# Products of ones through the first search of a linear-attention and balanced-expert kernel, with an older order of its attention loop

## The chip, the cores and the metric

The kernel runs on one core of a Trainium2 chip, in one launch. The metric is the device time of that launch in microseconds (us), compared by the median of several runs. A profile of one execution stands beside it. Engines are named as in the profile: PE (matrix products), DVE (vector), ACT (scalar), POOL (GpSimd) and SP, whose queue issues most transfers.

## The reference, cut to what matters

```python
# attention: q, k, v are (8, 8, 576, 64)
kv  = np.einsum('bhsd,bhse->bhde', k, v)
out = np.einsum('bhsd,bhde->bhse', q, kv)
rms = np.sqrt(np.mean(out * out, axis=-1, keepdims=True) + 1e-06)
x   = (out / rms * g_norm).transpose(0, 2, 1, 3).reshape(4608, 512)

# experts: w_gate (512, 8), w1 (8, 512, 1024), w2 (8, 1024, 512), cap = 576
logits = x @ w_gate
order = np.argsort(-logits.flatten())
for idx in order:                       # the best pair of token and expert first
    tok, e = idx // 8, idx % 8
    if assigned[tok] >= 0 or counts[e] >= cap: continue
    assigned[tok] = e; counts[e] += 1
for e in range(8):
    out[assigned == e] = np.maximum(x[assigned == e] @ w1[e], 0) @ w2[e]
```

Each expert takes exactly 576 tokens. Which ones is decided greedily over all pairs, so an expert's rows are known only when a threshold on the logits has been found at which it is full.

## The kernel before, in words

**Attention** (`prepare`, `tiles`). There are eight batches. `load` issues k, v and q of a batch in halves (`h`) of 576 KB on SP's queue; `paced` makes each load wait for the third one before it. `prepare(b)` is a generator with four or five parts, which makes what the tiles of batch `b` need: `sum_kv(r)` multiplies k and v of one pair of heads into `kv_ps` (four values of r), ACT and DVE bring the sum to `kv`, POOL copies it to `kvx`, PE turns it round (`t_ps`), ACT copies that to `kvt`, PE multiplies it with the gate (`w_ps`) and DVE copies the result into `kvx`. `turn_q(n)` (n from 0 to 4) transposes q into `qt`, copied from PSUM by DVE for n = 1 and 2 and by ACT otherwise. `again` issues the load for batch b + 2 into the buffers that have come free.

The main loop goes over the batches. A batch has four tiles of 128 tokens, an odd one also the tile that is split between it and the batch before. `one(t)` makes a tile: sixteen records of products into `o_ps` (two buffers), ACT squares it and copies it to `o_sb`, DVE sums the squares. After each tile comes the next part of `prepare(b + 1)`, so PE's order is tile, part, tile, part. `scale` and `logits` then give the norm and the logits of the batch; POOL scales the rows into `xo`, except those of the last batches (`own` false), which ACT scales after the loop (`late`, L529). `writes` holds the transfers of `xo` to `x_dram`. Here they are issued behind batches 4 and 5 and at the end. `chore` does pieces of the search's set-up (`early`) between tiles. In this stretch the orders of PE, DVE, ACT and SP are those of the program.

`ones(n)` gives PE n products of ones, 128x128 by 128x512 in bf16, whose result nobody reads. `warm(n)` is the same in the second pool of PSUM. Before, `ones` stands at the start (18), in batch 0's preparation (2, 6, 5), before `kv_ps` (2) and before some tiles of the first batches; `warm` stands behind the list of the first expert (20) and between its transposes.

**The first search** (`threshold(0)`, `assign_first`, `fetch(0)`). Six steps narrow the threshold. In each, PE counts, in 36 small products (L665), how many tokens are over each of 32 candidates; DVE finds the first full expert's place (L679, L681); PE adds it over the partitions (L686, "the number"); DVE makes from it the next midpoint (L691), for the first steps digits (L316) and comparisons (L322), later candidates (L708) and comparisons (L336), in three thirds, so that PE can begin on the first. `lowest` puts two products more (L630, L633) behind the number in two of the steps. `assign_first` then adds up who is taken (L748, L763), `fetch(0)` makes the list of rows (L931 to L950), POOL gathers them from `x_dram` (L971), PE transposes them (L1063) and the first expert's products begin (L1161).

**The experts.** For each expert the products of both layers, with the next expert's search interleaved in a planned order. The change does not touch this.

Of the kernel before, what the change touches and what calls it, by code (L numbers as in the profile page):

```python
# [26 lines left out]
def kernel(  # L27
# [63 lines left out]
    for b, order in enumerate(("kvqkvq", "kvkvqq")):  # L91
        for n, name in enumerate(order):
            load(name, b, int(name in order[:n]))
# [274 lines left out]
    def prepare(b):  # L368
# [4 lines left out]
        qt = att.tile([P, 2, NT, HP], FT, name="qt", tag="qt", bufs=2)  # L373
# [25 lines left out]
        def again(names, h):  # L399
            if b + 2 < B:  # L400
                for name in names:
                    load(name, b + 2, h)

        turns = [[0], [1], [2], [3], [4]] if b == 0 else [[], [0], [1, 2], [3], [4]]

        def turn_some():
            for n in turns.pop(0):
                turn_q(n)
                if n in (2, 4):
                    again("q", n // 2 - 1)  # L410

        if b > 0:
            ones(2, kv_ps[:, 0, :])
        sum_kv(0)
        sum_kv(1)
        again("kv", 0)
        if b == 0:
            ones(2)
        turn_some()
        yield  # L420
        if b == 0:
            ones(6)
# [10 lines left out]
        kvx = att.tile([P, H, W], FT, name="kvx", tag="kvx", bufs=2)  # L433
        for n in range(2):
            nc.gpsimd.tensor_copy(kvx[n * D:(n + 1) * D, :, 0:D], kv.rearrange("p r l d -> p (r l) d"))
        turn_some()
# [3 lines left out]
        if b + 1 == B:  # L440
            ones(3)
# [5 lines left out]
        turn_some()  # L447
        yield
        turn_some()
# [10 lines left out]
        turn_some()  # L460

    HELD = 6
    writes, late = [], []
    last_own = GC - R

    def tiles(c0, rows):
# [4 lines left out]
        xo = att.tile([P, T, H, D], FT, name="xo", tag="xo", bufs=HELD)  # L471
# [5 lines left out]
        def one(t, copies, fill, wait):  # L477
# [22 lines left out]
            if not wait:  # L500
                while copies:
                    copies.pop(0)()
# [39 lines left out]
    with tc.manual_schedule(engines={PE, DVE, ACTE, SPE}):  # L542
        ones(18)
        for _ in prepare(0):
            pass
        for b in range(B):
            parts = prepare(b + 1) if b + 1 < B else iter(())
            rows = [((b, j), (b, j + 2)) for j in (0, 1, 4, 5)]
            if b % 2:
                rows.append(((b - 1, R - 1), (b, R - 1)))  # L550
            one, scale, logits = tiles(b // 2 * R + b % 2 * (R // 2), rows)
            copies = []
            if b in choose_at:
                early(*choose_at[b])
            order = range(len(rows)) if b % 2 == 0 else [len(rows) - 1] + list(range(len(rows) - 1))
            for n, t in enumerate(order):
                one(t, copies, 1 if b < 3 and n in (0, 3) else 0, b + 1 == B and n == len(rows) - 2)
                next(parts, None)
                if b < 2 or b == 6 or n in (1, 3):
                    chore()  # L560
            for _ in parts:
                pass
            if b + 1 == B:
                while chores:
                    chore()
            scale()
            logits()
            if b < 4:
                chore()

            while b in (B - 4, B - 3) and writes:
                writes.pop(0)()
        early(27, GC)
        while chores:
            chore()
        for do in late:
            do()
        while writes:
            writes.pop(0)()
# [35 lines left out]
    for n, x in enumerate((-0.5, 1.0 / QP, 0.0)):  # L615
        nc.vector.memset(one_more[:, n:n + 1], x)

# [35 lines left out]
    def threshold(t, over, width, inv, mid):  # L653
# [3 lines left out]
        for s in range(NSTEP):  # L657
# [4 lines left out]
            if first:  # L662

                for c in range(GC):
                    nc.tensor.matmul(n_ps[0:QP, :, 0],  # L665
                                     lhsT=over[c // THIRD][:, c % THIRD],
                                     rhs=best[:, :, c], start=(c == 0), stop=(c == GC - 1))
            else:
                for c in range(0, GC, G):
                    nc.tensor.matmul(n_ps, lhsT=over[:, c:c + G].rearrange("p c n -> p (c n)"), rhs=best[:, :, c:c + G],  # L670
                                     start=(c == 0), stop=(c == GC - G))
# [14 lines left out]
            nc.tensor.matmul(kk, lhsT=ones_b, rhs=some, start=True, stop=True)  # L686
            exact = s + 1 >= DIGITS
# [45 lines left out]
    def assign_first(ends):  # L733
# [14 lines left out]
        nc.tensor.matmul(all_ps[:, 0:2].rearrange("p t e -> p (t e)"), lhsT=ones_b, rhs=sums, start=True, stop=True)  # L748
        edge = small("edge", GC)
# [13 lines left out]
        nc.tensor.matmul(all_ps[:, 2, 0:1], lhsT=before, rhs=turn_of[:, GC - 1:GC], start=True, stop=True)  # L763
        nc.vector.tensor_tensor(room, room, all_ps[:, 0], op=AL.subtract)
# [137 lines left out]
    def warm(times):  # L902
        w_ps = psm.tile([P, 512], FT, name="warm_ps", tag="y", bufs=2)
        for _ in range(times):
            nc.tensor.matmul(w_ps, lhsT=ones_b, rhs=wide, start=True, stop=True)

    def fetch(t, which, index, later):
# [25 lines left out]
        nc.tensor.matmul(a_ps[:, GC + 1:GC + 2], lhsT=prior, rhs=along[:, GC - 1:GC], start=True, stop=True)  # L933
        kn = know[:, t % 2]
# [16 lines left out]
        if t == 0:  # L951

            warm(20)
# [391 lines left out]
```

## Time and profile before

| what | us |
|---|---|
| median of 3 runs (650.66 to 658.63) | 651.92 |
| the profiled execution's own time | 650.66 |
| its span in the profile | 648.9 |
| PE busy in the span | 601.2 |
| DVE busy | 380.6 |
| POOL busy | 387.0 |
| ACT busy | 202.3 |
| last attention tile, start of its products | 113.61 |
| first count of the search's last nine columns (L665) | 121.68 |
| numbers (L686) of the six steps | 122.53, 125.37, 128.22, 131.07, 134.66, 138.78 |
| products of the list (L950) | 145.51 |
| first transposes of gathered rows (L1063) | 151.32 |
| first expert product (L1161) | 155.57 |

Times of instructions are counted from the start of the span. A line of the timeline gives the start, the duration, the engine, the line of the kernel, the operation, what it writes and reads, and in brackets how long the engine was idle before it and what ended that. Durations of single products on PE include their drain, so successive ones overlap, and what a product costs PE is the distance to the next one's start.

### The profile page before, as it was taken

Reading aid. Unit: us, or ns where it says so; the run is one execution under the profiler, and the core shown is the slowest. Engines: PE = TensorE matmul, PEld = TensorE weight load, DVE = VectorE, ACT = ScalarE, POOL = GpSimd, SP = SyncE. Lnnn points to the kernel's source line nnn. Section 1 sums busy time; section 2 is a strip of 40 time slices with the busy share of each in tenths; the row PEclk is TensorE's granted clock in tenths of the full one; section 3 lists DMA queues with packets and bytes.
Section 4 is the critical chain, followed back from the end, with each engine's and each line's share of the span. In section 5 each row is a group of like instructions: output and inputs, shape, how many; then the busy total and the mean of one; then the engine's idle time right before and its main releaser. Section 6 shows DMA issues by size and latency. Waiting matters only on the chain.

```text
span 648.9 us, 12775 instructions
## 1 busy us (share of the span) xinstructions
PE 601.2 (93%) x4918; PEld 464.2 (72%) x4932; DVE 380.6 (59%) x1242; ACT 202.3 (31%) x429; POOL 387.0 (60%) x403
## 2 busy tenths in 40 slices
PE   7889899438999999999999999999999999999993
PEld 4677777325787678777867786778678777867873
DVE  4466658767887678479658857966762052132101
ACT  1565656922321232123222312230233123122310
POOL 1136433006775598479738973877498579849822
PEclk9999999559999999999999999999999999999998
DMA  8999997428109105320821091017104420910001
GB/s 272 299 319 307 308 310 294 169 79 261 66 7 325 60 15 202 131 74 2 289 76 42 5 328 41 34 55 277 42 34 156 176 73 1 316 57 34 0 10 65
DMA packets 49884, 91.02 MB, mean 140 GB/s; under 512 B 3744, under 2 KB 20128, under 8 KB 49824
## 3 DMA queue, kind: packets, MB, share of 16 engines
q1 hardware_dynamic: 43200, 71.31, 32.0%
q0 software_dynamic: 5920, 18.88, 8.5%
q8 instruction: 39, 0.64, 0.4%
q14 instruction: 21, 0.17, 0.1%
q10 hardware_dynamic: 704, 0.02, 0.1%
HBM read 71.32 MB, written 18.87 MB: 139 GB/s over the span
## 4 chain that ended last, share of the span: by engine, by line
PE 78%; DVE 8%; issue 5%; DMA 4%; ACT 3%; POOL 2%; POOLq 0%; SPq 0%; DVEq 0%; ACTq 0%
PE x_ps L1161 13%; PE x_ps L1121 12%; PE z_ps L1161 9%; PE y_ps L1161 9%; PE y_ps L1121 8%; PE z_ps L1121 7%; PE o_ps L492 4%; PE y_ps L1223 4%; PE t_ps L1063 3%; DMA v_sb<-in_v_dram 3%; PE kv_ps L396 2%; PE qt_ps L381 2%; PE given_ps L670 1%; PE given_ps L665 1%; ACT sq L498 1%
## 5 line engine op out<-in xcount | busy, mean ns | idle before, releaser
L1166 ACT COPY h<-x_ps 128x288 f32<-128x288 f32 x93 | 37.2, 400 | 165.8 <-PE x_ps L1161 157.8
L1161 PE MATMUL x_ps<-xs,sw 128*128 128x288 f32 x248 | 71.4, 409 | 0.3 <-DVE xs L1076 0.3
L1088 POOL DMA_INDIRECT out_dram<-y_sb,outs x32 | 31.5, 985 | 57.5 <-DVE y_sb L1259 41.7
L1121 PE MATMUL x_ps<-tw,sh 128*128 128x256 f32 x256 | 61.7, 384 | 0.0
L1161 PEld LDWEIGHTS x_ps<-xs,sw 128*128 128x128 f32 x248 | 46.1, 190 | 13.3 <-issue 0.9
L1068 ACT ACTIVATE xt<-t_ps,g_col 128x512 f32<-128x512 f32 (+3 forms) x41 | 25.8, 635 | 91.3 <-PE t_ps L1063 83.6
L524 POOL TENSOR_TENSOR xo<-o_sb,inv 128x512 f32<-128x512 f32 x27 | 28.4, 1081 | 40.3 <-DVE inv L511 40.3
L1113 POOL TENSOR_TENSOR sh<-hid 128x512 f32<-128x512 f32 x32 | 40.7, 1271 | 19.7 <-ACT hid L1136 19.7
L1121 PEld LDWEIGHTS x_ps<-tw,sh 128*128 128x128 f32 x256 | 47.0, 190 | 7.5 <-issue 1.5
L1049 POOL TENSOR_TENSOR sw<-w_sb 128x256 f32<-128x256 f32 x64 | 46.9, 733 | 7.6 <-PE z_ps L1161 7.3
L1136 ACT ACTIVATE hid<-hid 128x576 f32<-128x576 f32 x64 | 43.8, 686 | 22.8 <-DVE hid L1175 12.6
L971 POOL DMA_INDIRECT xg<-x_dram,ids x40 | 38.0, 950 | 15.4 <-issue 9.9
L1199 POOL TENSOR_TENSOR tw<-w_sb 128x512 f32<-128x512 f32 x32 | 40.0, 1273 | 6.9 <-DMA w_sb<-in_moe_w_dram 6.9
L492 PE MATMUL o_ps<-kvx,qt 64*128 64x72 f32 (+1 forms) x640 | 39.2, 271 | 1.0 <-ACT o_sb L499 0.6
L492 PEld LDWEIGHTS o_ps<-kvx,qt 64*128 64x128 f32 (+1 forms) x640 | 34.1, 177 | 6.4 <-issue 4.5
L1161 PE MATMUL z_ps<-xt,sw 128*128 128x288 f32 x128 | 38.0, 414 | 0.0
L1161 PE MATMUL x_ps<-xt,w_sb 128*128 128x288 f32 x124 | 37.3, 415 | 0.6 <-ACT xt L1068 0.6
L503 DVE TENSOR_REDUCE ms<-sq 128x8 f32<-128x512 f32 x36 | 24.4, 683 | 22.3 <-ACT sq L498 22.2
L1161 PE MATMUL y_ps<-xt,w_sb 128*128 128x288 f32 x128 | 36.8, 408 | 0.0
L1161 PE MATMUL z_ps<-xs,sw 128*128 128x288 f32 x128 | 36.8, 409 | 0.0
L1161 PE MATMUL y_ps<-xs,w_sb 128*128 128x288 f32 x128 | 36.5, 407 | 0.0
L1253 ACT COPY u<-x_ps 128x512 f32<-128x512 f32 x24 | 14.0, 584 | 67.3 <-PE x_ps L1121 52.6
(307 smaller groups left out, 1324.5 us busy)
## 6 DMA issues: line engine op xcount, KB each, us to landing
w_sb<-in_moe_w_dram SPq DMA_DIRECT2D x32, 512.0 KB
w_sb<-in_moe_w_dram SPq DMA_DIRECT2D x8, 2048.0 KB
k_sb<-in_k_dram SPq DMA_DIRECT2D x16, 576.0 KB
v_sb<-in_v_dram SPq DMA_DIRECT2D x16, 576.0 KB
q_sb<-in_q_dram SPq DMA_DIRECT2D x16, 576.0 KB
x_dram<-xo SPq DMA_DIRECT2D x16, 512.0 KB
x_dram<-xo SPq DMA_DIRECT2D x4, 256.0 KB
xg<-x_dram,ids POOLq DMA_INDIRECT x40
```

The lines of the kernel that those rows point to most:

```text
L492: nc.tensor.matmul(o_ps[rows_at, rp, (2 * r2 + l) * W:(2 * r2 + l + 1) * W], lhsT=turned_q[bn][ks, l, block // 2:block // 2 + m].rearrange ...
L524: nc.gpsimd.tensor_tensor(xo[:, t], o_sb[:, t, :, 0:D], inv[:, t * H:(t + 1) * H].rearrange("p (h o) -> p h o", o=1).to_broadcast([P, H, D ...
L971: tokens = nc.gpsimd.indirect_dma_start(out=xg[0:nr], out_offset=None, in_=x_dram, in_offset=bass.IndirectOffsetOnAxis(ap=ids[0:nr, n:n + ...
L1049: in_order(nc.gpsimd.tensor_tensor(o, x, y, op=op))
L1088: put = nc.gpsimd.indirect_dma_start(out=out, out_offset=bass.IndirectOffsetOnAxis(ap=ids_of[t][0:nr, n:n + 1], axis=0), in_=y_sb[0:nr, :] ...
L1113: in_order(nc.gpsimd.tensor_tensor(o[:, ms], x[:, ms], y[:, ms], op=op))
L1121: nc.tensor.matmul(p_ps[:, n], lhsT=left[:, f, n * P:(n + 1) * P], rhs=right[:, f], start=first, stop=(f == FH - 1), skip_group_check=True)
L1136: nc.scalar.activation(both, both, ACT.Relu)
L1161: nc.tensor.matmul(p_ps, lhsT=lhs[:, r], rhs=rhs[:, r], start=(m in (1, 2, 4, 5) and r == 0), stop=(r == 1), skip_group_check=(m in (6, 7, ...
L1166: nc.scalar.copy(u, p_ps)
L1199: in_order(nc.gpsimd.tensor_tensor(o, x, y, op=AL.subtract))
L1223: nc.tensor.matmul(y_ps[l * nr:(l + 1) * nr], lhsT=hid[:, l * FH + f, a:a + nr], rhs=w2[:, l * FH + f, :], start=(f == 0), stop=(f == FH - 1))
```

## The change

It does two things. In the first search it puts products of ones wherever PE waits: seven behind the last attention tile, ten between the first 27 counts and the last nine, four behind each number and nine behind the last, three and five within the assignment, two behind the first products of the list and 24 in place of 20 behind the list. And it takes the attention loop in another order: the split tile comes last in its batch and not first; q of a batch is turned one part earlier, with one half of `kv_ps` per part (so `qt` and `kvx` have three buffers); every batch has one product of ones before its first tile and two before its fourth; batch 1 is loaded in the order k, v, q; the writes of x are issued behind each batch as soon as eight are pending; and only the last batch is scaled late by ACT.

```diff
-    for b, order in enumerate(("kvqkvq", "kvkvqq")):
-        for n, name in enumerate(order):
-            load(name, b, int(name in order[:n]))
+    for b in range(2):
+        for h in range(2):
+            for name in "kvq":
+                load(name, b, h)
...
-        turns = [[0], [1], [2], [3], [4]] if b == 0 else [[], [0], [1, 2], [3], [4]]
...
         if b > 0:
             ones(2, kv_ps[:, 0, :])
-        sum_kv(0)
-        sum_kv(1)
-        again("kv", 0)
-        if b == 0:
-            ones(2)
-        turn_some()
-        yield
-        if b == 0:
-            ones(6)
+        for r in range(2):
+            sum_kv(r)
+            if r:
+                again("kv", 0)
+            turn_q(r)
+            yield
         sum_kv(2)
         sum_kv(3)
         again("kv", 1)
...
-        turn_some()
         if b == 0:
             ones(5)
         yield
-        if b + 1 == B:
-            ones(3)
+        turn_q(2)
+        again("q", 0)
         t_ps = psa.tile([P, NP, D], FT, name="t_ps", tag="tr", bufs=2)
...
-        turn_some()
         yield
-        turn_some()
+        turn_q(3)
...
-        turn_some()
-
-    HELD = 6
+        turn_q(4)
+        again("q", 1)
+
+    LAG = 4
     writes, late = [], []
-    last_own = GC - R
+    last_own = GC - (R + 1) // 2
...
-            order = range(len(rows)) if b % 2 == 0 else [len(rows) - 1] + list(range(len(rows) - 1))
-            for n, t in enumerate(order):
-                one(t, copies, 1 if b < 3 and n in (0, 3) else 0, b + 1 == B and n == len(rows) - 2)
+            for t in range(len(rows)):
+                one(t, copies, {0: 1, 3: 2}.get(t, 0))
                 next(parts, None)
-                if b < 2 or b == 6 or n in (1, 3):
+                if b < 2 or t == 3 or b == 6 and t == 2:
                     chore()
             for _ in parts:
                 pass
             if b + 1 == B:
+                ones(7)
                 while chores:
                     chore()
             scale()
             logits()
-            if b < 4:
-                chore()
-
-            while b in (B - 4, B - 3) and writes:
+            if b < B - 1:
+                chore(2 if b == 6 else 1)
+
+            while len(writes) >= 2 * LAG:
                 writes.pop(0)()
...
+    def warm(times):
+        w_ps = psm.tile([P, 512], FT, name="warm_ps", tag="y", bufs=2)
+        for _ in range(times):
+            nc.tensor.matmul(w_ps, lhsT=ones_b, rhs=wide, start=True, stop=True)
...
                 for c in range(GC):
+                    if s == 0 and c == 27:
+                        warm(10)
                     nc.tensor.matmul(n_ps[0:QP, :, 0],
...
             nc.tensor.matmul(kk, lhsT=ones_b, rhs=some, start=True, stop=True)
+            if first:
+                warm(9 if last else 4)
...
         nc.tensor.matmul(all_ps[:, 0:2].rearrange("p t e -> p (t e)"), lhsT=ones_b, rhs=sums, start=True, stop=True)
+        warm(3)
...
         nc.tensor.matmul(all_ps[:, 2, 0:1], lhsT=before, rhs=turn_of[:, GC - 1:GC], start=True, stop=True)
+        warm(5)
...
+        if t == 0:
+            warm(2)
...
         if t == 0:
 
-            warm(20)
+            warm(24)
```

## The prediction

> **What bounds the kernel now.** I read the page's slices first, for the stages and the granted clock.
>
> ```profile
> span 648.9 us, 12775 instructions
> ...
> PE   7889899438999999999999999999999999999993
> ...
> DVE  4466658767887678479658857966762052132101
> ...
> PEclk9999999559999999999999999999999999999998
> ```
>
> A slice is 16.2 us. Slices 1 to 7 are the attention (to about 115 us), the two with clock 5 are the first search, and the rest is the experts' products, which the change leaves alone: everything it can win or lose lies before the first expert product at 155.57. So I take the part before in batches, and then in steps of the search. PE alone in the timeline, over the end of one attention batch:
>
> ```profile
> 65.91 0.66 PE L381 MATMUL qt_ps<-ident,q_sb 128*128 128x128 f32 x4
> 67.19 0.66 PE L381 MATMUL qt_ps<-ident,q_sb 128*128 128x128 f32 x4 [0.62 <-ACT kvt L446]
> 67.77 1.11 PE L492 MATMUL o_ps<-kvx,qt 64*128 64x72 f32 x16
> 68.82 0.66 PE L381 MATMUL qt_ps<-ident,q_sb 128*128 128x128 f32 x4
> 69.41 0.65 PE L456 MATMUL w_ps<-gw,kvt 128*64 128x16 f32 x16
> 70.44 0.44 PE L381 MATMUL qt_ps<-ident,q_sb 128*128 128x128 f32 x2 [0.39 <-DVE kvx L458]
> ```
>
> From start to start a tile costs 1.05 us, four turns of q 0.585, w_ps 0.60, t_ps 0.39, half of kv_ps 0.655 a pair. Apart from two waits (0.62 and 0.39) PE is never idle: a batch of four tiles is 4x1.05 + 2.62 + 2.64 + 0.39 + 0.60 + 0.47 (two products of ones) = 10.9, and with the waits 11.9. The first tiles of batches 4 and 5 stand at 71.85 and 83.77, 11.92 apart. From batch 2 on the attention is bound by PE, and each product put in PE's queue costs its time.
>
> The search is a ring between DVE and PE:
>
> ```profile
> 125.37 0.16 PE L686 MATMUL given_ps<-some,ones_b 128*128 128x3 bf16 x1 [0.43 <-DVE some L681]
> ...
> 125.58 0.28 DVE L691 TENSOR_SCALAR mid<-given_ps,cells,mid 128x1 f32<-128x1 f32 x1 [0.26 <-PE given_ps L686]
> 125.89 0.32 DVE L316 TENSOR_SCALAR digit<-mx,mid,inv 128x72 bf16<-128x72 f32 x1
> 126.24 0.90 DVE L322 TENSOR_TENSOR over_c<-digit,marks 128x384 bf16<-128x384 bf16 x3
> 126.65 1.03 PEld L665 LDWEIGHTS <-over_c 128*32 128x32 bf16 x36 [1.10 <-DVE over_c L322]
> ```
>
> Between the number (L686) and the next counts (L665) PE has 1.28 us free; that is the gap the new products fill. The clock, by the microsecond (columns PE, PEld, DVE, ACT, POOL, granted clock, DMA share, GB/s):
>
> ```profile
> 112.00:113.00 1.00, 1.00 (x20) 0.92 (x18) 0.93 (x2) 0.64 (x3) 0.00 (x0) 1.00 1.01 371
> 113.00:114.00 1.00, 0.62 (x13) 0.48 (x10) 0.69 (x1) 1.00 (x3) 0.00 (x0) 1.00 1.01 371
> 114.00:115.00 1.00, 1.00 (x14) 0.84 (x12) 0.69 (x1) 0.06 (x1) 0.00 (x0) 0.62 1.01 371
> ...
> 148.00:149.00 1.00, 1.00 (x5) 0.40 (x4) 0.87 (x5) 0.00 (x0) 0.85 (x1) 0.81 0.60 193
> ```
>
> It falls at 114.25, while PE is still working, and is back at 148.38, some 2.3 us into the twenty products of ones.
>
> **What the half clock costs now: little.** PE's counts start 27 ns apart in the search and 25 ns apart (L670) at full clock; from the last count to the DVE instruction behind it is 0.21 us in both, and from L686 to L691 0.20 against 0.21 to 0.24. So a full clock saves 36 x 2 ns = 0.07 in each of three steps on digits, nothing in the steps through L336, where DVE's thirds of 0.50 us set the pace, 0.1 at the first count, and 0.4 at the last attention tile (1.44 us at 113.61 against 1.05). That is 0.7 at most. The gathers are not helped: the ones behind the list now end at about the time the first rows land (transposes from 151.3), and 24 x 0.216 = 5.2 us from 145.86 end at 151.1.
>
> **Attention, part by part.** (1) The loop's order. In the changed one tile 0 is followed by half of kv_ps and one turn, tile 1 likewise, tile 2 by kv_ps 1.31, tile 3 by turn 2, t_ps, turn 3, w_ps, turn 4. The last stretch has nothing to lie beside in a batch of four. With tile 3's end as zero: turn 2 to 0.585, t_ps to 0.975; ACT does the square (0.17), the copy (0.66), then kvt (1.19 to 1.56), so turn 3 runs from 1.62 to 2.2, w_ps to 2.8, turn 4 waits for ACT's copy of turn 3 (2.35 to 2.95) and ends at 3.3. In a batch of five the split tile stands behind t_ps: turn 3 from 1.98, w_ps to 3.15, turn 4 behind DVE's kvx (3.43 to 3.64) to 4.0.
> (2) Ones. 0.31 us before tile 0, 0.47 before tile 3, 0.47 before kv_ps, by their rows' starts (46.24 to 46.56; 97.73 to 98.20). Before, only batches 0 to 2 had fills.
> Sums: four tiles 0.31 + 4x1.05 + 0.47 + 4x0.655 + 2x0.585 + 0.47 + 3.3 = 12.54; five 13.24. The old ones, from first tile to first tile, for batches 1 to 6: 13.3, 12.6, 13.0, 11.92, 12.98, 12.05. Differences -0.06, -0.06, +0.24, +0.62, +0.26, +0.49.
> (3) Loads. q is turned one step earlier, and for batch 2 that meets the load: the SP queue issues load n once n-3 has landed, and by that q's first half lands at about 35.9 where the new order wants it at 34.6: +1.3. Later loads are ahead by 2 us or more. In batch 0, with k, v, q in that order and no 2 + 6 ones at its start, the first tile of batch 1 comes 0.85 earlier (v lands at 25.8; kv_ps, ones, tile, 3.3: 32.1 against 32.94).
> (4) Writes. Three x writes of 512 KB go to the SP queue ahead of batch 7's six loads; at 305 GB/s these 1.6 MB move the landing of q's first half from about 94.5 (read off the issue three places behind it) to 99.6, and it is wanted at 100.8. Hidden by 1.2 us; what of that is missing would go on the path.
> (5) Batch 6's scaling moves from ACT (32 x 0.24 = 7.7 us behind 116.86) to POOL (4 x 1.05), idle there. ACT's tail is not on the chain: x lands at 137, the gathers start at 147.88. Nothing.
> (6) Batch 7 is paced by ACT's two passes per tile; its full clock saves 0.2 of the 0.4 above.
> Sum for the attention: -0.85 - 0.06 + 1.3 - 0.06 + 0.24 + 0.62 + 0.26 + 0.49 - 0.2 = +1.7. Bounds: without the load stall and with the loop-end waits (0.85 a batch of four, 0.55 of five) all hidden -3.8; with batch 7 two us late +4.
>
> **The new products in the search.** At full clock one is 0.216 us and all fit: 4 are 0.86 of 1.28, 9 are 1.94 of 2.8 (138.78 to 141.56), 3 are 0.65 of 1.40, 5 are 1.08 of 1.74, 2 are 0.43 of 0.8. Then they cost nothing and save 0.5. At half clock (0.43 each) 4 take 1.72, and the counts start 0.53 late; 9 delay L748 by 1.2, 5 delay L931 by 0.5; the lowest logit's products (L630, L633) then stand on the path, 0.3 each.
>
> Which clock? The window that lost it, from 110.84 to 114.25, held 47 records of o_ps and nothing else. That is 2.9 tiles of 1.05 us on 64 of the array's 128 rows: 0.45 of the array. In the search 0.86 us of full products in a step of 2.85 is 0.30, and between the ten products at the start and the next counts are over 2 us with none. By that row the clock falls again within the first two steps. Once it is at half, 1.72 + of 3.4 us are busy, and it may return: it came back with 0.8, and stayed down with 0.2 (counts alone). I take it to toggle, half of the price: 0.53 x 1.5 + 0.3 + 0.6 + 0.25 - 0.4 = +1.5; bounds -0.5 and +3.8.
>
> The Trainium skill, TensorE: Matmul & The Clock Gate, Part 1, What's actually happening, names an idle window of about 3.4 us as what throttles PE; by it no gap here is long enough, the clock would hold and the sum would be that of the first rival. The fall at 114.25 with PE at work speaks against it as the whole rule.
>
> **Total.** +1.7 + 1.5 = +3.2 on the profiled execution's 650.66, 653.9. That run is the lowest of three; I add the same to their median, 651.92: 655.1, put at 655.0.
>
> **Rivals.**
> The clock holds through the search: +1.7 - 0.5 = +1.2, 653.1. For it: PE is busy in some way in nearly every microsecond of the steps. Against it: the window at 110.84.
> Faster: the waits at the end of each batch disappear, because ACT and DVE reach kvt and qt sooner than I let them. Price 3 x 0.85 + 3 x 0.55 = 4.2, attention -2.5; with the clock held -3.0, 648.9; with it toggling -1.0. It decides from the point where more than 3.2 of the 4.2 is hidden. For it: ACT is busy only 7 of 12 us a batch. Against it: in a batch of four nothing else stands in PE's queue.
> DMA becomes the bound: writes among the loads make batch 7 wait 2 to 3 us, and all else as forecast: 657.5. For it: DMA share 0.92 to 0.96 to 95 us. Against it: the 1.2 us of slack and PE's slower batches.
>
> **How the numbers follow.** Forecast 0.50, clock holds 0.25, faster 0.15, DMA 0.10. The forecast's own range is 652 to 658; to the rivals and the runs' own spread it is 649 to 660. Two per cent, about what this kernel's measurement can tell, is 13 us, and no case reaches it: faster 0.01, within 0.96, slower 0.03.
>
> **What would show it.** First tiles of batches 2, 4, 6 at about 46.65, 72.4, 98.2 (before 46.24, 71.85, 96.75), the last attention product 1.7 later than 115.05, waits of PE for kvt and qt at each batch's end, one wait for q near 35. Granted clock 1.00 past 115 and falling between 121 and 126; PE waiting for nothing between L686 and the counts where it is half. I am wrong if the clock stays 1.00 to the gathers, if the batches are shorter than before, or if anything behind the first expert product moves against its start by over 1 us.

## The result, and the profile after

The changed kernel takes 660.26 us (median of 22 runs, 657.33 to 669.57), the kernel before 651.53 on the same chips: ratio 1.0139, interval 1.0115 to 1.0162, about 9 us. A second set of four runs gave 658.08, ratio 1.0137 (1.0120 to 1.0153). The forecast was +3.2 us, 655.0; the measured median lies just above the upper end of its range, 660.0. Ratios and intervals, here and below, leave out executions that took over 1.5% longer than the fastest of the same kernel; medians and ranges have all. Two executions were profiled: the first took 663.41 us (span 661.5), the second, called `after_again` below, 656.76 (span 654.9). The median lies between them.

The slices of the first profile:

```profile
span 661.5 us, 12874 instructions
...
PE   7989999688999999999999999999999999999994
...
DVE  4456667767688588568757956975782053123201
...
PEclk9979999858999999999999999999999999999998
```

Three things differ in the row of the clock: a 7 in the third slice, inside the attention; an 8, a 5 and an 8 where before had two 5s (the clock comes and goes around the search); and the search lies half a slice later. PE is busy 24 us longer (625.2 against 601.2); its products of ones take 23 us longer (42.7 against 19.7).

Milestones, in us from the start of the span:

| | before | after | after_again |
|---|---|---|---|
| first tile of batch 2 | 46.6 | 49.9 | 46.3 |
| first tile of batch 4 | 71.8 | 75.9 | 72.2 |
| first tile of batch 6 | 96.7 | 101.6 | 98.0 |
| first tile of batch 7 | 108.8 | 114.3 | 110.7 |
| end of the last tile | 115.05 | 123.11 | 120.00 |
| start of the last nine columns of the first count | 121.68 | 130.73 | 127.95 |
| first and last number | 122.53, 138.78 | 131.57, 149.10 | 128.79, 145.25 |
| products of the list | 145.51 | 156.94 | 152.81 |
| first expert product | 155.57 | 166.87 | 162.59 |

In the second profile 7.0 us are lost by the first expert product, and in three places: 1.9 up to the first tile of batch 7, 3.1 within batch 7 (9.3 us from its first tile to the end of its last, before 6.25), 2.1 from there to the first expert product. The first profile has the same three (the last two at 2.5 and 3.2) and 3.6 us more in batch 1.

**The loops.** PE over the end of a batch, to be laid beside the one shown of before:

```profile
71.80 0.66 PE L382 MATMUL qt_ps<-ident,q_sb 128*128 128x128 f32 x4
72.39 0.46 PE L433 MATMUL t_ps<-ident,kv 64*128 64x64 f32 x4
72.78 0.98 PE L481 MATMUL o_ps<-kvx,qt 64*64 64x72 f32 x32
73.69 0.66 PE L382 MATMUL qt_ps<-ident,q_sb 128*128 128x128 f32 x4
74.27 0.65 PE L444 MATMUL w_ps<-gw,kvt 128*64 128x16 f32 x16
75.30 0.44 PE L382 MATMUL qt_ps<-ident,q_sb 128*128 128x128 f32 x2 [0.38 <-DVE kvx L446]
```

This is batch 3, with five tiles: turn 2, t_ps, then the split tile, which fills the time that a batch of four has nothing for, turn 3, w_ps, and the one wait for DVE's kvx (0.38, before 0.39). PE sets the pace here as before.

**Batch 7.** The timeline of four engines, cut to the lines that matter:

```profile
116.14 4.25 POOL L513 TENSOR_TENSOR xo<-o_sb,inv 128x512 f32<-128x512 f32 x4 [4.06 <-ACT sq L487]
...
116.95 0.27 DVE L303 TENSOR_REDUCE code_mx<-pick 128x9 f32<-128x72 f32 x1
117.26 1.12 DVE L305 TENSOR_TENSOR best<-pick,code_mx 128x72 bf16<-128x72 f32 x1
118.29 2.22 DVE L337 TENSOR_TENSOR over_c<-mx,cand 128x192 bf16<-128x192 f32 x2
120.43 2.08 DVE L492 TENSOR_REDUCE ms<-sq 128x8 f32<-128x512 f32 x3
...
121.20 0.60 ACT L487 ACTIVATE sq<-o_ps 128x512 f32<-128x512 f32 x1 [3.51 <-DVE ms L492]
...
122.38 0.73 PE L481 MATMUL o_ps<-kvx,qt 64*64 64x72 f32 x32 [2.97 <-ACT o_sb L488]
```

Read it from the bottom. PE stands 2.97 us before the last tile because ACT has not copied the tile two before it out of PSUM; ACT stands 3.51 because DVE has not summed the squares in the buffer it wants; DVE comes to those sums only at 120.43, because two pieces of the choice stand ahead of them in its queue. L305 takes 1.12 us and L337 1.1 us apiece. Before they took 0.23 and 0.26 (L304 and L336 there). What lies beside them is POOL's scaling of batch 6, from 116.14 to 120.39.

**Behind the last tile.**

```profile
123.04 2.83 PE L363 MATMUL ones_ps<-wide,ones_b 128*128 128x512 bf16 x6
...
125.98 0.24 DVE L599 COPY held_ps<-rise 128x72 f32<-128x72 f32 x1 [1.49 <-PE ones_ps L363]
126.13 0.39 DVE L497 RECIPROCAL inv<-rt 128x40 f32<-128x40 f32 x1
```

DVE's copy L599 writes a PSUM tile of the next pool, whose place the seven products of ones still use (the row has six of them; a record is missing). It waits for their end, and L497, the first step to the last batch's logits, is queued behind it. At half clock the products end at 125.9, and all that leads to the first count waits with them. It is the half clock that makes them late: in the five profiles where the seven ran at full clock (`search_alone`, `scale_on_act`, `products_held`, `chores_early`, `chores_early_fit`, below), this copy waits 0.39 us for ACT, as before, and 6.64 to 6.67 us go by from the last tile to the last nine columns (before 6.64; here 7.62, in the second profile 7.95).

**In the search**, from one number to the next counts:

```profile
134.41 0.16 PE L682 MATMUL given_ps<-some,ones_b 128*128 128x3 bf16 x1 [0.43 <-DVE some L677]
...
134.43 1.87 PE L610 MATMUL warm_ps<-wide,ones_b 128*128 128x512 bf16 x4
134.61 0.28 DVE L689 TENSOR_SCALAR mid<-given_ps,cells,mid 128x1 f32<-128x1 f32 x1 [0.26 <-PE given_ps L682]
...
135.28 0.90 DVE L323 TENSOR_TENSOR over_c<-digit,marks 128x384 bf16<-128x384 bf16 x3
...
136.23 0.58 PE L624 MATMUL f_ps<-ident,low 128*1 128x128 f32 x2
...
136.61 0.54 PE L661 MATMUL given_ps<-best,over_c 128*32 128x8 bf16 x13
```

The counts start 2.20 us after the number; before it was 1.28. Four products at half clock last until 136.2, then come the products of the lowest logit, then the counts, whose first third DVE had ready at 135.64. The numbers are 3.80 and 3.90 us apart here (2.85 before).

**The clock** (columns: PE, PEld, DVE, ACT, POOL, granted clock, DMA share, GB/s):

```profile
36.00:38.25 2.25, 2.09 (x47) 1.88 (x51) 1.07 (x7) 0.89 (x2) 2.02 (x3) 0.97 1.03 311
38.25:45.08 6.83, 6.50 (x115) 5.33 (x110) 2.31 (x9) 2.53 (x5) 0.00 (x0) 0.51 0.94 318
...
120.40:123.00 2.60, 0.62 (x32) 0.58 (x32) 2.12 (x5) 1.63 (x3) 0.00 (x0) 1.00 0.58 221
123.00:127.00 4.00, 3.84 (x42) 1.75 (x36) 2.25 (x9) 1.89 (x4) 0.00 (x0) 0.57 0.01 4
130.40:133.80 3.40, 2.33 (x49) 1.66 (x50) 2.44 (x10) 3.40 (x16) 0.00 (x0) 0.98 0.39 154
133.80:137.20 3.40, 2.96 (x35) 1.43 (x32) 2.08 (x9) 3.11 (x14) 0.00 (x0) 0.50 0.39 151
```

It falls three times: at 38.09, behind a wait of PE for q (1.67 us, ended at 36.16 by the load); at 123.43, behind the wait in batch 7; and at 133.67, in the second step of the search, from where it stays at half to 154.15. The second profile has no fall at q. It falls at 117.85, during the wait in batch 7, and in the search at 131.50 and, after 3.4 us at full clock, again at 138.33, to 148.57.

### The profile page after: what moved, and what is told of

It is laid out like the page before. It is cut to its first block, busy times and chain, and to the rows that moved or that the text cites. A ratio compares the mean times of both kernels' runs of the same rounds, so it can differ in the third digit from the quotient of the medians.

```text
span 661.5 us, 12874 instructions
## 1 busy us (share of the span) xinstructions
PE 625.2 (95%) x4977; PEld 472.6 (71%) x4999; DVE 385.8 (58%) x1242; ACT 194.8 (29%) x397; POOL 390.9 (59%) x407
## 4 chain that ended last, share of the span: by engine, by line
PE 81%; DVE 7%; issue 4%; DMA 2%; ACT 2%; POOL 1%; POOLq 0%; SPq 0%; DVEq 0%; ACTq 0%
PE x_ps L1158 13%; PE x_ps L1118 11%; PE z_ps L1158 9%; PE y_ps L1158 8%; PE y_ps L1118 7%; PE z_ps L1118 7%; PE o_ps L481 5%; PE y_ps L1220 4%; PE kv_ps L397 3%; PE t_ps L1060 3%; PE warm_ps L610 2%; PE qt_ps L382 2%; DMA v_sb<-in_v_dram 2%; PE given_ps L666 1%; PE given_ps L661 1%
## 5 line engine op out<-in xcount | busy, mean ns | idle before, releaser
L1158 PEld LDWEIGHTS x_ps<-xs,sw 128*128 128x128 f32 x248 | 46.1, 190 | 13.3 <-issue 0.9
L513 POOL TENSOR_TENSOR xo<-o_sb,inv 128x512 f32<-128x512 f32 x31 | 32.9, 1090 | 30.3 <-DVE inv L500 17.0
L481 PEld LDWEIGHTS o_ps<-kvx,qt 64*128 64x128 f32 (+1 forms) x640 | 34.2, 180 | 12.7 <-issue 7.8
L425 POOL COPY kvx<-kv 64x512 f32<-64x512 f32 x16 | 9.7, 607 | 44.4 <-DVE kv L419 24.8
```

The costliest lines, as they stand in the source:

```text
L481: nc.tensor.matmul(o_ps[rows_at, rp, (2 * r2 + l) * W:(2 * r2 + l + 1) * W], lhsT=turned_q[bn][ks, l, block // 2:block // 2 + m].rearrange ...
L513: nc.gpsimd.tensor_tensor(xo[:, t], o_sb[:, t, :, 0:D], inv[:, t * H:(t + 1) * H].rearrange("p (h o) -> p h o", o=1).to_broadcast([P, H, D ...
L1158: nc.tensor.matmul(p_ps, lhsT=lhs[:, r], rhs=rhs[:, r], start=(m in (1, 2, 4, 5) and r == 0), stop=(r == 1), skip_group_check=(m in (6, 7, ...
```

## The experiments

Each ratio is taken against the kernel before on the same chip. Unless said otherwise the medians are of 4 to 12 runs.

**The two halves of the change.** `search_alone` is the kernel before with the change's products in the search (and the seven behind the last tile):

```diff
             if b + 1 == B:
+                ones(7)
...
+                    if s == 0 and c == 27:
+                        warm(10)
...
             nc.tensor.matmul(kk, lhsT=ones_b, rhs=some, start=True, stop=True)
+            if first:
+                warm(9 if last else 4)
...
+        warm(3)
...
+        warm(5)
...
+            warm(2)
...
-            warm(20)
+            warm(24)
```

> The kernel before, with only the change's new products of ones: 7 behind the last tile, 10, 4 a number, 9, 3, 5, 2 and 24. Theory (the loss has four parts: about 3 us around batch 1, from q's wait and a fall of the clock; 2 in the later batches; 2.5 in batch 7, where POOL scales rows while DVE compares; 3 in the search): 2 to 4 us slower than before, last tile's end where it was, near 115, and the first expert product 2 to 4 us later. Rival (the products of ones are the whole loss, since they stand in front of the counts at half clock): 8 us slower or more. Second rival (they help where the attention leaves them alone): not slower than before.

656.51 us, ratio 1.0075 (1.0045 to 1.0104), +4.9. From the last tile to the first expert product 42.7 us went by, before 40.5. Those 40.5 hold a wait of 0.8 us between the fifth and the sixth number that no other profile has; without it, as in `attention_alone` and `pool_scale` below, the stretch takes 39.6, so the products cost 3.1 us there. One more microsecond of the 4.9 lies outside the span: all six executions took 2.6 to 3.0 us longer than their spans, those of before about 1.8. No run shows why. The profiled execution was the longest of the six (662.84 us), with the clock at half from 38.17 to 58.65, in the attention, which this kernel leaves as it was.

`attention_alone` is the changed kernel without any of these products, all else as changed.

> The changed kernel without the search's new products (20 behind the list as before). Theory of four parts: 5 to 8 us slower than before, the last tile ending near 122, and the search as long as before, 40 to 41 us from the last tile to the first expert product. Rival (the search's products are the whole loss): within 1 us of before.

656.65 us, ratio 1.0104 (1.0057 to 1.0151), its runs far apart (653.49 to 662.88). In the profile the first tile of batch 7 comes 2.4 us late and batch 7 takes 9.1 us; the search is as before, 39.6 us. So both halves cost, each more than forecast.

**Two places of the attention.** `scale_on_act` gives batch 6's scaling back to ACT in the changed kernel:

```diff
-    last_own = GC - (R + 1) // 2
+    last_own = GC - R
```

> The changed kernel, but batch 6 scaled by ACT behind the loop as in the kernel before, so that POOL is idle during batch 7. Theory (DVE's comparisons take 1.1 us each in place of 0.26 while POOL scales, and the sums of squares queue behind them): 2 to 3 us faster than the changed kernel, ACT waiting for DVE in batch 7 no longer than 1 us (3.5 in the changed one), batch 7 from its first tile to its last end 6.2 us in place of 8.7. Rival (the comparisons stand in a bad place of DVE's queue whatever POOL does): less than 0.8 us faster.

The pieces of the choice stand where the change puts them, and only POOL is idle. Batch 7 took 6.2 us in its profile, and L305 and L337 were back at 0.24 and 0.26 us. The time did not follow: 661.03 us, ratio 1.0172 (1.0133 to 1.0212). Its profiled run was the fastest of six (656.64 to 667.02). In it PE had a wait of 1.3 us in batch 5 that the changed kernel does not have, and one of 1.1 for kvt in batch 6 that is 0.5 there. The same line also puts off one of ACT's copies in batch 6 (L489, `if own or t != T - 2`), which may be the second of these waits; that was not tested. The other five took 1.9 to 2.8 us longer than their spans, before about 1.8. Why its runs are so slow is not settled.

`ones_at_q` puts six products of ones ahead of the first turn of q for batch 2, into the wait for the load:

```diff
+            if b == 2 and r == 0:
+                ones(6)
             turn_q(r)
```

> The changed kernel with six products of ones (1.3 us) put into the wait for batch 2's first half of q (1.7 us), before its first turn. Theory (the wait lets the clock fall for two windows, 38.3 to 45.1, and that costs some 1.7 us beside the wait's 1.7): the clock stays 1.00 to 120 us, and batch 2's first tile comes 1.5 to 2 us earlier than in the changed kernel (49.9). Rival (the clock's fall is hidden behind the loads): first tile within 0.4 us of 49.9, whatever the clock.

658.69 us, ratio 1.0115 (1.0087 to 1.0142). The clock held there and batch 2 began at 46.4, but so it did (45.7 to 46.3) in `attention_alone`, `scale_on_act` and `after_again` without the six products. The fall at 38 us belongs to single executions, also of kernels with the old loop (`search_alone` at 38.17, `products_fit` and `pool_scale` at 25.3), and this ratio's interval overlaps the changed kernel's: the gain is not shown.

**How much fits into the search.** `products_held` is the kernel before with more products, laid into the gaps:

```diff
-                one(t, copies, 1 if b < 3 and n in (0, 3) else 0, b + 1 == B and n == len(rows) - 2)
+                one(t, copies, 1 if b < 3 and n in (0, 3) or b + 1 == B and n else 0, b + 1 == B and n == len(rows) - 2)
...
+                    if s == 0 and c == 27:
+                        warm(17)
...
+            if first:
+                warm(2)
             nc.tensor.matmul(kk, lhsT=ones_b, rhs=some, start=True, stop=True)
...
                 next(of_floor, None)
+                warm((5, 4, 5, 6, 6, 11)[s])
```

(and 5, 6 and 3 in the assignment and ahead of the list, 7 behind the last tile, 24 behind the list).

> The kernel before, with more products of ones in the search than the change has, laid into the gaps that the trace of before shows: 7 behind the last tile, 17 between counts 27 and 28, two ahead of each number, 5, 4, 5, 6, 6 and 11 behind the six numbers (behind the tensor products of the lower bound, not ahead of them), 5, 6 and 3 within the assignment, 24 behind the list, and one with each tile of batch 7 but the first. Theory (the clock goes by how much of the array works in a window of 3.41 us; it fell at 0.40 and less and stood at 0.45 and more): every window between 114 and 150 us comes to 0.45 or more, the granted clock stays 1.00 there, no number waits for products (7 x 0.213 us fit into the 2.85 us of a step), and from the last tile to the first expert product 39.0 to 39.7 us go by against 40.5 before; the time is that of before within 1.5 us: full clock is worth almost nothing in the search, because a count took 27 to 29 ns at half and 25 ns at full clock. Rival 1 (idle gaps decide, however full the window is): the clock falls within the first two numbers, each number then waits for 9 products of 0.43 us, and the search takes 45 us or more: +5 us on the time. Rival 2 (full clock does speed up the search): the stretch falls to 37 us or less.

The windows of the profile, with the same columns as above:

```profile
114.00:118.00 4.00, 4.00 (x41) 2.64 (x40) 2.28 (x4) 2.99 (x6) 0.00 (x0) 1.00 0.01 3
...
126.00:130.00 4.00, 4.00 (x66) 2.27 (x62) 2.47 (x13) 4.00 (x18) 0.00 (x0) 1.00 0.36 135
...
142.00:146.00 4.00, 3.40 (x19) 1.38 (x18) 3.07 (x18) 0.00 (x0) 0.00 (x0) 1.00 0.00 0
```

The clock is 1.00 from the attention to the gathers, and the stretch takes 39.9 us. The time: 650.91 us against 650.54, ratio 1.0000 (0.9959 to 1.0041). A full clock through the whole search is worth nothing that this comparison can tell. Some of the products stand in the way themselves (the second and third interval of the numbers are 2.93 and 3.15 us, against 2.85), so a few tenths could be hidden.

`products_fit` is `search_alone` with its products cut to what fits at half clock:

```diff
-                warm(9 if last else 4)
+                warm(5 if last else 2)
...
-        warm(5)
+        warm(3)
...
-            warm(2)
+            warm(1)
```

> The kernel before with the search's products of the change, but so few behind each number that they fit in the gap at half clock as well: 2 (5 behind the last number) in place of 4 and 9, 3 and 3 within the assignment in place of 3 and 5, 1 in place of 2 ahead of the list. Theory (the price of the search's products is that 4 x 0.43 us at half clock are longer than the 1.28 us from a number to the next counts): the clock is at half from the second number on as in the change, the numbers are 2.85 us apart again, and from the last tile to the first expert product 39.7 to 40.5 us go by (42.7 with the change's products): time within 1.5 us of before. Rival (the price lies in the products before the first counts and round the list, or in PE's queue being busy at all): 42 us or more, time +3 to +5 us as with the change's products alone.

651.14 us, ratio 1.0012 (0.9987 to 1.0037), against 1.0075 with the change's numbers. The clock was at half from behind the first number on. From the first to the last number it took 15.8 us (`search_alone` 17.5), from there to the list 6.7 (7.8), and the whole stretch 40.8, of which 0.9 is the seven products at half clock again. (The profiled execution, 663.87 us, lost its time ahead of this stretch: batch 7 began at 122.4.) So the price of the products behind the numbers and in the assignment lies in their size.

**DVE beside POOL.** `chores_early` is the changed kernel with batch 6's pieces of the choice behind its tiles:

```diff
-                if b < 2 or t == 3 or b == 6 and t == 2:
+                if b < 2 or t == 3 or b == 6:
                     chore()
...
-                chore(2 if b == 6 else 1)
+                chore(0 if b == 6 else 1)
```

> The changed kernel with one thing undone: batch 6's four pieces of the choice go behind its four tiles, as before the change, and none behind its logits; batch 6's scaling stays on POOL. Theory (batch 7's loss of 2.5 us is DVE's two-input operations, L305 and L337, which take 1.12 and 2 x 1.1 us while POOL scales, against 0.23 and 2 x 0.26 us without, and stand in DVE's queue ahead of batch 7's first sums): from the first tile of batch 7 to the end of the last 6.2 to 6.6 us (8.7 in the changed kernel), with those operations back at 0.2 to 0.3 us each, and 2 to 2.5 us off the time. Rival 1 (POOL slows every operation of DVE): 8 us or more again, because batch 7's sums of squares are then what is slow. Rival 2 (the pieces cost the same wherever they stand): batch 6 grows by what batch 7 sheds, and the last tile ends at most 0.5 us earlier.

```profile
101.53 2.22 DVE L337 TENSOR_TENSOR over_c<-mx,cand 128x96 bf16<-128x96 f32 x2
...
100.31 5.34 POOL L513 TENSOR_TENSOR xo<-o_sb,inv 128x512 f32<-128x512 f32 x5 [5.08 <-DMA x_dram<-xo]
...
109.54 0.23 DVE L305 TENSOR_TENSOR best<-pick,code_mx 128x72 bf16<-128x72 f32 x1
109.68 0.52 DVE L337 TENSOR_TENSOR over_c<-mx,cand 128x192 bf16<-128x192 f32 x2
...
113.72 1.27 DVE L492 TENSOR_REDUCE ms<-sq 128x8 f32<-128x512 f32 x2
...
112.92 4.14 POOL L513 TENSOR_TENSOR xo<-o_sb,inv 128x512 f32<-128x512 f32 x4 [3.77 <-ACT sq L487]
...
118.61 0.24 DVE L599 COPY held_ps<-rise 128x72 f32<-128x72 f32 x1 [0.39 <-ACT o_sb L488]
```

653.56 us, ratio 1.0058 (1.0028 to 1.0089): more off than expected. Batch 6's pieces of the choice (from 109.54) cost what they cost before; POOL still scales while batch 7 runs, and the sums of squares beside it take their usual 0.6 to 0.7 us, so POOL does not slow all of DVE. Batch 7 takes 5.8 us. And since its array no longer idles, the clock stays full past the last tile: the seven products are over in 1.69 us, and L599 waits for ACT (0.39) and not for them. That is a second microsecond, in the next stage.

One thing more is in these lines. The pieces before those, L337 at 101.53, run in batch 6 beside POOL's scaling of batch 5 and take 1.1 us apiece, here as in the changed kernel. Yet batch 6 takes 12.7 us in both, as long as batches 2 and 4: PE sets the pace there, and DVE has room. Being slow beside POOL costs time only where the queue behind it is waited for, as in batch 7.

`pool_scale` is the one line turned round, in the kernel before: batch 6 scaled on POOL, where no piece of the choice stands behind its logits.

> The kernel before with one line changed: batch 6's scaling on POOL in place of ACT, as the change has it. Theory (only a two-input operation of DVE at the same time pays): before has no such operation behind batch 6's logits until the sums of batch 7 are over, so batch 7 takes 6.3 to 6.6 us as before, and the time is that of before within 1 us; ACT's 32 products of 0.24 us, gone from behind the last tile, were off the chain. Rival 1 (POOL slows all of DVE): batch 7 takes 8 us or more, +2 us. Rival 2 (ACT's products stood on the chain): 1 to 3 us faster than before.

651.42 us, ratio 1.0003 (0.9970 to 1.0035); batch 7 took 6.2 us. Moving the scaling costs nothing by itself, and ACT's products behind the loop were not on the chain. Only the two together cost: POOL's scaling and two-input operations of DVE in the same stretch, ahead of sums that ACT and PE wait for.

**The parts put together.** `change_fit` is the changed kernel with only the search's products cut as in `products_fit`.

> The changed kernel with the search's products cut to what fits at half clock (2 behind a number, 5 behind the last, 3 and 3 in the assignment, 1 ahead of the list), all else as changed. Theory: from the last tile to the first expert product 40 to 41 us in place of 43.75, 1.5 to 3.5 us off the time of the changed kernel on the same chip; batch 7 stays at 8.7 us. Rival (the search's price was a matter of where the clock's windows fell): within 1 us of the changed kernel.

```profile
131.09 0.16 PE L682 MATMUL given_ps<-some,ones_b 128*128 128x3 bf16 x1 [0.44 <-DVE some L677]
...
131.12 1.02 PE L610 MATMUL warm_ps<-wide,ones_b 128*128 128x512 bf16 x2
...
132.44 1.15 PE L661 MATMUL given_ps<-best,over_c 128*32 128x8 bf16 x36
```

654.66 us, ratio 1.0081 (1.0064 to 1.0098), 3.4 below the changed kernel on the same chip. From the number to the counts 1.35 us go by, at half clock, where the four products made it 2.20.

`after_again`, the changed kernel itself:

> The changed kernel itself, once more, for a second profile. What repeats belongs to the change, what does not to the execution. If batch 7 (8.7 us), the search (43.75 us) and the late start of DVE in the second expert (1.3 us) are the change's, all three come back within 0.3 us, 1 us and 0.3 us. The fall of the clock behind the first wait for q (38 to 45 us) need not: three of the four kernels with that order had none. Time 658 to 662.

Batch 7 (9.3 us, 0.5 more than in the first profile) and the search (42.6) came back; the clock's fall at 38 us did not, and neither did a late start by 1.3 us in the second expert (from the first product of its second layer to that of the next expert's 62.39 us in the first profile, 61.06 in this one and in before). These two belong to the execution.

`chores_early_fit` has both cures:

> The changed kernel with two parts undone at once: batch 6's four pieces of the choice behind its tiles, and so few products in the search that they fit at half clock (2 behind a number, 5 behind the last, 3 and 3 in the assignment, 1 ahead of the list). What is left of the change is its order of the attention, its two more products of ones in each batch, POOL's scaling and the products before the first counts and behind the list. If the parts found so far (the price of products that don't fit, and DVE beside POOL) and the 1.9 us of the attention's loops are all of the change's 8.7 us, then the first tile of batch 7 comes 2.0 to 2.6 us later than before, batch 7 takes 5.7 to 6.2 us, the search 40 to 41 us, and the time is 651.5 to 652.8, 1 to 2 us over before. Rival (something else of the change costs as well, as in the second expert, where the changed kernel's profile lost 1.3 us to a late start of DVE): 654 us or more.

652.36 us, ratio 1.0037 (1.0005 to 1.0069). Its profile was 1.1 us later at batch 1 (33.15) than `after_again`, so its first tile of batch 7 is at 112.5, later than I expected; from batch 1 to batch 7 it is 79.4 us (before 75.6, `after_again` 78.6). Batch 7 took 5.8 us and the search 39.8. The four kernels make a square (us over the kernel before, by the ratios times 650):

| | pieces late, as changed | pieces early |
|---|---|---|
| the change's products in the search | 8.9 | 3.8 |
| products that fit | 5.3 | 2.4 |

So the change's 8.9 us are about 2.4 for what is left, and 6.5 for the two faults together. Singly they are 3.6 and 5.1, 8.7 in sum. That they overlap is plausible, but the times do not show it: each ratio is uncertain by 1 to 2 us, and the four come from three chips.

**What is left** I put down to the products of ones in the loops. `few_fills` is `chores_early_fit` with

```diff
-                one(t, copies, {0: 1, 3: 2}.get(t, 0))
+                one(t, copies, {0: 1, 3: 2}.get(t, 0) if b < 3 else 0)
```

> As chores_early_fit, and without the change's three products of ones in each attention loop from batch 3 on (one ahead of tile 0, two ahead of tile 3). Theory (TensorE paces these loops, its rows show no gap longer than 0.5 us there, so each product costs its 0.21 us): batches 3 to 6 take 0.4 to 0.65 us less each, the first tile of batch 7 comes at 108.8 to 109.6 us, and the time is 649.5 to 650.5, 0.5 to 1.5 us below the kernel before. Rival 1 (the loops' extra length is their order, not the products): the loops stay, 651.5 to 652.8 us, with no difference to chores_early_fit. Rival 2 (without the products a window of the attention comes below 0.40 of the array): the granted clock falls within batches 3 to 6, and most runs are at 654 us or more.

```profile
80.00:83.40 3.40, 2.63 (x28) 2.03 (x26) 2.02 (x4) 1.81 (x4) 1.21 (x2) 0.98 0.94 260
83.40:86.80 3.40, 3.40 (x34) 2.79 (x34) 1.37 (x6) 1.18 (x3) 0.00 (x0) 0.50 0.99 378
```

Its median is 653.57, its runs 647.62 to 669.11; the ratio, 1.0010 (0.9975 to 1.0045), overlaps that of `chores_early_fit`. Its fastest runs (647.62, 648.89, 649.29) lie about 2 us below the fastest of `chores_early_fit` (649.88, 651.07, 651.09) and level with the fastest of before (647.68), but a few fast runs prove nothing. The profile bears the first theory out by half: the fourth tile of batches 3, 4 and 6 comes 0.5 us earlier in its batch than in `chores_early_fit`; but batch 3, the only one of batches 3 to 6 that ran at full clock throughout, is just 0.2 us shorter (12.87 against 13.06), because other waits of PE come instead. In the profiled run the clock fell at 83.24, with PE busy for 77% of the window, and again at 110.55, as the second rival said; five of the twelve runs, not most, took 654 us or more. Four took over 658 us, and none of the twelve of `chores_early_fit` did. That the loops' products cost up to 2 us and buy steadiness is likely, not shown, and the 2.4 us that are left stay open. No version tried here beats the kernel before.

## Why the prediction was right or wrong

**Right: the loops.** Forecast for the first tiles of batches 2, 4 and 6: 46.65, 72.4, 98.2; the second profile has 46.3, 72.2, 98.0. Batch by batch, from 2 to 6, the loop took 12.7, 13.3, 12.7, 13.1 and 12.7 us against 12.54 and 13.24 in turn. The wait for q, put at 1.3, was 1.67 and 1.10. Part of the match is luck: the 46.24 that the forecast takes for before is the product of ones ahead of the tile, which itself begins at 46.56, so batch 2 came earlier than in before where +0.4 had been forecast, and the slightly longer loops made up for it. The clock's fall behind the wait (batch 1 took 3.6 us more in one profile of the nine with that order) was not in the sum; it should have stood in the range. The writes that go ahead of batch 7's loads were hidden, as worked out: PE waited for no load there.

**Wrong: step (5), "Nothing".** I costed the scaling's move on ACT, the engine it leaves, and on POOL, the engine it goes to. I did not ask which DVE instructions would then run beside POOL. The trace of before shows the price, where POOL scaled batch 5 from 99.95 to 105.23 (99.95 + 5.28):

```profile
99.95 5.28 POOL L524 TENSOR_TENSOR xo<-o_sb,inv 128x512 f32<-128x512 f32 x5 [8.22 <-DVE inv L511]
...
103.68 0.63 DVE L299 TENSOR_TENSOR pick<-lg,mx 128x72 f32<-128x72 f32 x1
104.34 0.97 DVE L300 TENSOR_TENSOR pick<-pick,code 128x72 f32<-128x72 f32 x1
...
108.29 0.23 DVE L304 TENSOR_TENSOR best<-pick,code_mx 128x72 bf16<-128x72 f32 x1
108.43 0.52 DVE L336 TENSOR_TENSOR over_c<-mx,cand 128x192 bf16<-128x192 f32 x2
```

Operations of one size, 0.63 and 0.97 us beside POOL and 0.23 without. The diff moves two chores behind batch 6's logits, exactly into POOL's new stretch, and I never costed the chores' move at all. By these rows three operations at 0.4 to 0.7 us more make 1.2 to 2.2 us; measured were 2.5 and 3.1 in batch 7.

**Wrong with it: step (6).** Batch 7 is not paced by ACT in the changed kernel but by DVE's queue ahead of the sums, and its wait cost the clock (117.85 in the second profile), which step (6) had at full. The bound "with batch 7 two us late +4" came nearest (the last tile ends 4.95 us later in the second profile), but it was kept as a bound and given no mechanism.

**Wrong in size: the search.** That the clock would fall within the first two steps was right: it did so in all six profiles with the change's numbers of products. That it would toggle, which halved the price, was right in two of them (`after_again`, `chores_early`); in the other four, the first profile among them, it stayed at half for 20.5 us, past the last number. So the term "half of the price" was too small. Terms, forecast against the two profiles:

| term | forecast | after | after_again |
|---|---|---|---|
| last tile to last nine columns of the first count | 0 | +1.0 | +1.3 |
| first to last number | +1.1 | +1.3 | +0.2 |
| last number to list | +0.85 | +1.1 | +0.8 |
| list to first expert product | 0 | -0.1 | -0.3 |

The first row was left out: I saw the seven products behind the last tile as filling an idle PE and did not name who waits for the PSUM that they write. The second row holds more than it shows, because the profiled execution of before had a wait of 0.8 us of its own between the fifth and the sixth number (4.12 us, against 3.33 to 3.41 in the other profiles), for which its trace shows no cause; against a step without it the numbers cost 1.0 to 2.1. Each digit step at half clock with a product of the lowest logit cost 0.95 to 1.05, the forecast's 0.53 plus 0.3 and a little. The forecast's saving of 0.4 at full clock stands in no row and was not seen. Part of it rested on a wrong comparison: the 25 ns of L670 belong to products of another shape (32 columns, not 8), and the counts themselves start 27 ns apart at full clock too (median, `products_held`).

**Rivals.** "The clock holds" did not happen, and `products_held` shows that it would have gained nothing to speak of. "Faster" and "DMA" did not happen. One of the signs of being wrong came in the first profile only: behind the first expert product it took 494.7 us, before 493.3; the second took 492.3. The evidence for the clock's fall was read a little high: the window up to 114.25, put at 0.45 of the array by the tiles' times, comes to 0.39 by the columns streamed (below), and windows of 0.40 to 0.45 kept the clock in every profile.

## What to carry to other kernels

Filler work is sized for the slow clock, not the fast one: if it fits only at full clock, it fails just when the clock has fallen. When a step is moved to another engine, list what runs beside it in its new stretch, and look up in the trace what those instructions take beside that engine. And ask of filler too who waits for the buffer it writes.

## What the runs showed of the hardware that was not expected

**DVE beside POOL.** In batch 7 operations of DVE with two tensors from SBUF took 1.1 to 1.2 us beside POOL's scaling, and 0.23 to 0.35 without. It is not one price: L299 and L300 took 0.63 and 0.97 beside it in before, and an L305 at 101.32 in `chores_early` 0.29. Reductions, with one tensor, took the same 0.6 to 0.7 us in both cases. The Trainium skill, SBUF — State Buffer, Who interferes with whom, says that a DVE instruction with two SBUF inputs contends with a GpSimd instruction that reads SBUF, and one with a single input (outside the modes that use both ports) does not. The traces agree in both, and the 1.1 us is about the length of one of POOL's four scalings (4.25 us for four).

**The clock is not only a matter of idle windows.** I added up what share of the array's cells the recorded products used (rows by columns, over 128 by 128, times the columns streamed, twice for fp32, over 2400 a microsecond; a 512-column bf16 product starts every 0.216 us at full clock, a 288-column fp32 one every 0.243) in windows of 3.413 us that end where the clock falls. The window's length is read off the traces: the clock's stretches at half last 3.41, 6.83, 13.66, 20.48 or 34.13 us and the like, whole multiples of it. In the 14 profiles it fell 27 times between 18 and 160 us, always after a window of 0.39 or less, also with PE busy most of the time: 0.39 (before, to 114.25), 0.34 (after, to 38.09), 0.37 (few_fills, to 83.24, PE busy 77%). After windows above 0.39 it never fell; between 0.33 and 0.39 it fell in some and stood in others, and since some records are missing from a trace the limit may be sharper than this. `products_held` had 0.45 or more in every window of the search.

**A full clock bought little.** With half of it the search took 39.6 us (`attention_alone`, `pool_scale`), with all of it 39.9 (`products_held`): counts and numbers wait for DVE, and the counts start 27 ns apart (median) at half clock in before and at full clock in `products_held`.
